# Eight uneven pieces of the first modulation weights in place of six

## The chip, the core and the metric

The kernel runs on one core of one Trainium2 chip. The core has five engines that run their own instruction streams: TensorE (PE, with its weight loads, PEld), VectorE (DVE), ScalarE (ACT), GpSimd (POOL) and SyncE (SP). Sixteen DMA engines bring data from HBM to the on-chip memory, SBUF, which has 128 partitions; here SP alone issues these transfers. The metric is the device time of one execution in microseconds.

## The reference

One token passes through a transformer block whose normalisations are modulated by a condition `c`. Everything is float32; H = 32 heads, 8192 cached keys and values of 192 numbers a head, D = 640.

```python
mod = (_silu(c) @ w_mod).reshape(c.shape[0], 6, 1, -1)
sa, ca, ga, sb, cb, gb = (mod[:, 0], mod[:, 1], mod[:, 2], mod[:, 3], mod[:, 4], mod[:, 5])
h = _layernorm(x, axis=-1) * (1 + ca) + sa
x = x + ga * _A_ref(h, A_k_cache, A_v_cache, A_wq, A_wo)   # attention of one query over the cache
h = _layernorm(x, axis=-1) * (1 + cb) + sb
x = x + gb * _B_ref(h, B_w1, B_b1, B_w2, B_b2)             # squared-relu feed-forward
```

The cache is 2 x 32 x 8192 x 192 x 4 bytes, 403 MB, and is read once. Together with the weights 451.83 MB come in.

## The kernel before

The host lays the inputs out as the transfers want them. Keys, values and the slices of `wq` and `wo` that go with them are cut by `plan()` into 53 chunks of at most 64,512 bytes a partition; each chunk is one transfer over 128 partitions, the last one two. Three buffers of this size (the pool `strm`) go round. SP's program is the list of transfers in the order written: `wm0`, the uneven pieces, chunks 0 and 1 (`load(0)`, `load(1)`), chunk 2 once the first buffer is free, and from then on `load(n + 3)` at the end of the work on chunk n; behind the chunks the remaining modulation weights (`wm1`), `w1` and `w2`, in pieces. In between, for each chunk, DVE multiplies the keys with the query (L273) and adds up the products (L281, with POOL's help at L399), PE forms the weighted sums of values (L322).

The first buffer holds, in columns, the modulation weights for the first normalisation (`wm0`: shift and scale, 2 x 640 outputs over 640 inputs, in KB = 5 groups of 128 inputs), the first slice of `wq` and some small vectors. A part of the fifth group, 480 of its 1280 columns for each of its 128 inputs, is not in this rectangle. Each of these 128 strips of 480 numbers stands at one of up to seven places (SX = 7 slots) of one of up to 64 partitions at the end of the same buffer, `wm0x_t`. DVE and POOL fill that region with zeros first (L120, L121), and then a table `XP` says where strips go. Its entries are (first partition, number of rows, slots): an entry (a, k, n) is one transfer to the k partitions a, a + 4, a + 8 and so on, each a row of n strips of 1920 bytes (L125). The host packs the values of `c` in the same way, so that zero meets zero where no strip is.

`mod(0, 2, ...)` then forms the shift and the scale on PE: the regular part at L198, the seven slots at L204. These feed the normalisation, the first query (`query(0, ...)`, L254), and with it DVE's first multiply.

SP's transfers report their landing on eight completion counters, DMAHW0 to DMAHW7 in the built program, taken in turn. A transfer that gets a counter which an earlier transfer has used carries a wait for that earlier one's landing. SP works through its list in order: what waits there holds up all that stands behind it.

Of the kernel before, what the change touches and what calls it, by code (L numbers as in the profile page):

```python
# [38 lines left out]
EXTRA = {"o": WO, "q": WQ}  # L39
SLOT = 84 * DH  # L40
SX = 7
XP = ((0, 3, SX), (1, 3, SX), (2, 3, SX), (3, 3, SX), (32, 3, SX), (33, 5, 5))
WX = 3 * DG
W0 = KB * 2 * D - WX
VPC = 5
# [48 lines left out]
def block_kernel(ctx: ExitStack, tc: tile.TileContext, kv, wm0, wm0x, wm1, w1, w2, out):  # L94
# [28 lines left out]
    r = 0  # L123
    for a, k, n in XP:
        nc.sync.dma_start(wm0x_t[a:a + 4 * k:4, :n * WX], wm0x[r:r + k, :n * WX])  # L125
# [395 lines left out]
```

## Time and profile before

| | us |
|---|---|
| median of 3 runs (1052.56 to 1052.58) | 1052.57 |
| span of the profiled execution, first to last instruction | 1050.6 |
| median less span: what lies around the profiled instructions | 2.0 |
| DVE busy in the span | 826.2 |
| PE busy in the span | 486.7 |
| POOL busy in the span | 190.5 |
| ACT busy in the span | 44.9 |

No time of the profiled execution other than its span is listed. The page gives busy time by engine, 40 slices of the span, the DMA queues, the chain of work that ended last, and groups of instructions. The chain is followed back from the last instruction: at each step to what released it. A transfer's "us to landing" runs from its issue on SP until its landing is known, and so includes the time that it stands in the rings of the DMA engines behind earlier transfers. KB on the page are 1024 bytes; MB and GB/s are decimal.

### The profile page before, as it was taken

What the parts mean: (1) busy time and instruction counts of PE and PEld (TensorE: products, weight loads), DVE (VectorE), ACT (ScalarE), POOL (GpSimd) and SP (SyncE); (2) the same over time, 40 slices, a digit from 0 to 9 for tenths busy, and PEclk for the clock granted to TensorE, in tenths of its full rate; (3) what the DMA queues carried; (4) which work ended last, traced back from release to release, by engine and by line L of the source; (5) the groups of instructions that cost most, each with busy time, mean ns of one, the idle gap of its engine ahead of it and who ended that gap; (6) DMA issues with size and microseconds to landing.
All of it is one profiled execution on the core that took longest, in us unless ns stands there. A gap on an engine that the chain in (4) does not pass through costs nothing.

```text
span 1050.6 us, 5178 instructions
## 1 busy us (share of the span) xinstructions
PE 486.7 (46%) x2130; PEld 133.8 (13%) x2130; DVE 826.2 (79%) x405; ACT 44.9 (4%) x122; POOL 190.5 (18%) x61
## 2 busy tenths in 40 slices
PE   3253334455352363436353356345446346435287
PEld 1010001111010010101011011001001011001023
DVE  1799878876959969888697895999887977988812
ACT  0100000000000000000000000000000000000001
POOL 1113121121212211212121121122211211211200
PEclk9676576777675686767677687686777767768689
DMA  9999999999999999999999999999999999999997
GB/s 406 432 433 432 431 440 442 436 436 430 433 432 432 435 440 433 432 429 434 432 433 435 435 431 434 432 438 432 438 437 431 432 430 430 432 435 440 420 432 336
DMA packets 9142, 452.14 MB, mean 430 GB/s; under 512 B 1032, under 2 KB 1036, under 8 KB 1420
## 3 DMA queue, kind: packets, MB, share of 16 engines
q1 hardware_dynamic: 9120, 451.83, 99.4%
q8 instruction: 16, 0.26, 0.1%
q14 instruction: 6, 0.05, 0.0%
HBM read 451.83 MB, written 0.00 MB: 430 GB/s over the span
## 4 chain that ended last, share of the span: by engine, by line
DMA 56%; DVE 30%; PE 12%; ACT 1%; issue 0%; SPq 0%; DVEq 0%; ACTq 0%
DMA chunk<-in_kv 53%; DVE chunk L273 16%; DVE sc L281 12%; PE ps_o L322 6%; PE ps_q L254 2%; PE att_a L354 2%; DMA w_t<-in_w 2%; DMA wm_t<-in_wm 1%; DVE os L336 1%; DVE om L334 1%; PE att_a L356 0%; ACT p L305 0%; PE ps_mx L297 0%; PE ps_mod L198 0%; PE ps_mod L204 0%
## 5 line engine op out<-in xcount | busy, mean ns | idle before, releaser
L273 DVE TENSOR_TENSOR chunk<-chunk,qb 128x8064 f32<-128x8064 f32 (+19 forms) x81 | 419.6, 5211 | 126.7 <-DMA chunk<-in_kv 121.5
L281 DVE TENSOR_REDUCE sc<-chunk 128x25 f32<-128x4800 f32 (+21 forms) x109 | 333.8, 3096 | 0.4
L399 POOL TENSOR_TENSOR chunk<-chunk 128x1824 f32<-128x1824 f32 (+9 forms) x51 | 187.4, 3675 | 801.3 <-DVE chunk L273 552.2
L322 PE MATMUL ps_o<-chunk,p 128*32 128x512 f32 x1536 | 287.1, 716 | 68.8 <-DMA chunk<-in_kv 59.4
L297 PE MATMUL ps_mx<-ident,mp 128*128 128x128 f32 x32 | 14.6, 457 | 350.4 <-DVE mp L295 350.4
L322 PEld LDWEIGHTS ps_o<-chunk,p 128*32 128x32 f32 x1536 | 66.0, 128 | 265.1 <-issue 181.4
L354 PE MATMUL att_a<-chunk,oW 128*32 128x512 f32 x96 | 64.2, 824 | 44.9 <-ACT oW L352 44.9
L254 PE MATMUL ps_q<-chunk,ln_h 128*128 128x512 f32 x110 | 66.4, 764 | 25.9 <-DMA chunk<-in_kv 25.9
L297 PEld LDWEIGHTS ps_mx<-ident,mp 128*128 128x128 f32 x32 | 5.7, 177 | 379.5 <-DVE mp L295 310.8
L305 ACT ACTIVATE p<-sc,nm 128x256 f32<-128x256 f32 x32 | 16.2, 508 | 650.2 <-DVE nm L299 650.2
L254 PEld LDWEIGHTS ps_q<-chunk,ln_h 128*128 128x128 f32 x110 | 26.4, 251 | 63.6 <-issue 34.4
L334 DVE TENSOR_TENSOR om<-ps_o,mask 96x512 f32<-96x512 f32 x32 | 21.6, 675 | 8.9 <-PE ps_o L322 8.9
L299 DVE TENSOR_REDUCE nm<-ps_mx 128x1 f32<-128x128 f32 x32 | 9.3, 292 | 19.4 <-PE ps_mx L297 19.4
L336 DVE TENSOR_REDUCE os<-om 96x64 f32<-96x512 f32 x32 | 21.8, 682 | 1.1
L354 PEld LDWEIGHTS att_a<-chunk,oW 128*32 128x32 f32 x96 | 12.1, 141 | 81.3 <-ACT oW L352 47.6
L344 DVE TENSOR_REDUCE oT<-ps_oT 128x3 f32<-128x96 f32 x16 | 4.0, 248 | 20.9 <-PE ps_oT L340 20.9
L310 PE MATMUL ps_sum<-ident,wide 128*128 128x128 f32 x16 | 7.4, 466 | 22.4 <-ACT wide L308 22.4
L340 PE MATMUL ps_oT<-ident,os 96*128 96x96 f32 x16 | 5.0, 314 | 27.0 <-DVE os L336 27.0
L198 PE MATMUL ps_mod<-wm_t,silu 128*32 128x480 f32 (+2 forms) x78 | 9.0, 602 | 14.4 <-DVE silu L180 14.4
L356 PE MATMUL att_a<-chunk,oW 128*96 128x384 f32 x32 | 14.5, 534 | 0.0
L352 ACT ACTIVATE oW<-oT,r 128x96 f32<-128x96 f32 x16 | 5.9, 372 | 174.6 <-DVE oT L344 174.6
L255 ACT ACTIVATE qb<-ps_q 128x512 f32<-128x512 f32 x12 | 7.2, 598 | 132.0 <-PE ps_q L254 132.0
(79 smaller groups left out, 99.8 us busy)
## 6 DMA issues: line engine op xcount, KB each, us to landing
chunk<-in_kv SPq DMA_DIRECT2D x38, 8064.0 KB, 35.4
chunk<-in_kv SPq DMA_DIRECT2D x11, 8000.0 KB, 36.9
chunk<-in_kv SPq DMA_DIRECT2D x2, 7872.0 KB
chunk<-in_kv SPq DMA_DIRECT2D x1, 6144.0 KB, 22.7
wm_t<-in_wm SPq DMA_DIRECT2D x1, 4480.0 KB
wm_t<-in_wm SPq DMA_DIRECT2D x1, 4257.0 KB, 12.5
chunk<-in_kv SPq DMA_DIRECT2D x1, 3264.0 KB
chunk<-in_kv SPq DMA_DIRECT2D x1, 3072.0 KB
```

Source lines behind the costliest of these rows:

```text
L254: nc.tensor.matmul(ps, h1[:, b:b + 1].to_broadcast([P, P]), w[:, b], start=(b == 0), stop=(b == KB - 1))
L273: nc.vector.tensor_mul(pr, pr, q[:, None, :].to_broadcast([P, b - a, DH]))
L281: nc.vector.tensor_reduce(sc[:, a % SRING:a % SRING + b - a], src[:, a - first:b - first], axis=AX.X, op=ALU.add)
L297: nc.tensor.transpose(ps[:, :P], mp.to_broadcast([P, P]), ident)
L299: nc.vector.tensor_reduce(nm, ps[:, :P], axis=AX.X, op=ALU.max, negate=True)
L305: nc.scalar.activation(p, s[:, :, None].to_broadcast([P, NPOS, 32 // E]), AF.Exp, bias=nm, accum_out=sp[:, h % 2:h % 2 + 1])
L322: nc.tensor.matmul(ps_t[h][32 * g:32 * (g + 1)], p[:, E * j:E * (j + 1)].rearrange("p e r -> p (e r)"), t[:, g], start=(j == 0), stop=last)
L334: nc.vector.tensor_mul(om[:n], ps_t.pop(h)[:n].rearrange("p (d e) -> p d e", e=E), mask[:n, None, :].to_broadcast([n, ED, E]))
L336: nc.vector.tensor_reduce(os_[:n, h % 2], om[:n], axis=AX.X, op=ALU.add)
L354: nc.tensor.matmul(att_a[96:, :512], oW[:, j], w[:, j, :512], start=(first and j == 0), stop=(last and j == NV - 1))
L356: nc.tensor.matmul(att_a[:96, :NV * (D - 512)], oW.rearrange("p j r -> p (j r)"), w[:, :, 512:], start=first, stop=last)
L399: nc.gpsimd.tensor_add(half, half, kt[:, m:, DH // 2:])
```

## The change

The table `XP` gets eight entries in place of six, with other partitions, row counts and slot counts. The 128 strips are the same, and so are `wm0`, the tile, and the matmuls; the host packs by the same table.

```diff
 SX = 7
-XP = ((0, 3, SX), (1, 3, SX), (2, 3, SX), (3, 3, SX), (32, 3, SX), (33, 5, 5))
+XP = ((32, 8, 4), (33, 4, 1), (0, 3, SX), (1, 3, SX), (2, 3, SX), (3, 3, SX), (20, 2, 2), (12, 1, 4))
 WX = 3 * DG
```

Before, five transfers of three rows with seven strips (13,440 bytes a row) and one of five rows with five strips (9,600 bytes). Now one of eight rows with four strips (7,680 bytes), one of four rows with one strip (1,920), four of three rows with seven strips (13,440), one of two rows with two strips (3,840) and one of one row with four strips (7,680).

The first place where this moves instructions is the start of SP's list. `wm_t<-in_wm` is `wm0`, `wm_t<-in_wm0x` are the uneven pieces, the shapes are partitions x numbers, and in brackets stands what a transfer waits for; of before:

```order
1 L122 DMA wm_t<-in_wm 128x8514
2 L125 DMA wm_t<-in_wm0x 3x3360 [waits DVE_49,Pool_49]
3 L125 DMA wm_t<-in_wm0x 3x3360 x4
4 L125 DMA wm_t<-in_wm0x 5x2400
5 L240 DMA chunk_100<-in_kv 128x12288
6 L240 DMA chunk_102<-in_kv 128x16000 [waits DMAHW0_49]
7 L240 DMA chunk_178<-in_kv 128x16128 [waits DMAHW3_49,DMAHW4_49,DMAHW2_49,DMAHW5_49,DMAHW1_49,DMAHW6_49,DVE_49,PE_49]
8 L240 DMA chunk_193<-in_kv 128x16128 [waits DMAHW7_49,DVE_49]
```

and of the change:

```order
1 L122 DMA wm_t<-in_wm 128x8514
2 L125 DMA wm_t<-in_wm0x 8x1920 [waits DVE_49,Pool_49]
3 L125 DMA wm_t<-in_wm0x 4x480
4 L125 DMA wm_t<-in_wm0x 3x3360 x4
5 L125 DMA wm_t<-in_wm0x 2x960
6 L125 DMA wm_t<-in_wm0x 1x1920 [waits DMAHW0_49]
7 L240 DMA chunk_102<-in_kv 128x12288 [waits DMAHW1_49]
8 L240 DMA chunk_104<-in_kv 128x16000 [waits DMAHW2_49]
9 L240 DMA chunk_180<-in_kv 128x16128 [waits DMAHW4_49,DMAHW5_49,DMAHW3_49,DMAHW6_49,DMAHW0_49,DMAHW7_49,DVE_49,PE_49]
10 L240 DMA chunk_195<-in_kv 128x16128 [waits DMAHW1_49,DVE_49]
```

Before, `wm0` and the pieces take counters 0 to 6, chunk 0 takes counter 7 without a wait, and chunk 1 is the first to meet a used counter. Now `wm0` and seven pieces take all eight; the one-row piece waits for counter 0, `wm0`, chunk 0 for counter 1, the eight-row piece, and chunk 1 for counter 2, the four-row piece. From here on all transfers stand in the same order as before, each with a counter two further on.

The second place is PE's start, where L204 reads the pieces; of before:

```order
1 L198 MATMUL ps_mod_104<-wm_t,silu 32x320 [waits DMAHW0_49,DVE_49]
2 L198 MATMUL ps_mod_104<-wm_t,silu 32x320 x17
3 L198 MATMUL ps_mod_104<-wm_t,silu 32x160
4 L204 MATMUL ps_mod_104<-wm_t,silu 32x160 [waits DMAHW4_49,DMAHW5_49,DMAHW3_49,DMAHW6_49,DMAHW2_49,DMAHW1_49]
5 L204 MATMUL ps_mod_104<-wm_t,silu 32x320
```

and of the change:

```order
1 L198 MATMUL ps_mod_106<-wm_t,silu 32x320 [waits DMAHW0_49,DVE_49]
2 L198 MATMUL ps_mod_106<-wm_t,silu 32x320 x17
3 L198 MATMUL ps_mod_106<-wm_t,silu 32x160
4 L204 MATMUL ps_mod_106<-wm_t,silu 32x160 [waits DMAHW4_49,DMAHW5_49,DMAHW3_49,DMAHW6_49,DMAHW2_49,DMAHW7_49,DMAHW1_49,DMAHW0_49]
5 L204 MATMUL ps_mod_106<-wm_t,silu 32x320
```

The matmuls are the same; the first one at L204 waits for all eight pieces, where it waited for six.

## The prediction

> **What bounds the kernel now.** I read the page first: the 40 slices, the queues and the chain of waits.
>
> ```profile
> DMA  9999999999999999999999999999999999999997
> ...
> q1 hardware_dynamic: 9120, 451.83, 99.4%
> q8 instruction: 16, 0.26, 0.1%
> ...
> DMA 56%; DVE 30%; PE 12%; ACT 1%; issue 0%; SPq 0%; DVEq 0%; ACTq 0%
> DMA chunk<-in_kv 53%; DVE chunk L273 16%; DVE sc L281 12%; PE ps_o L322 6%; PE ps_q L254 2%; PE att_a L354 2%; DMA w_t<-in_w 2%; DMA wm_t<-in_wm 1%; DVE os L336 1%; DVE om L334 1%; PE att_a L356 0%; ACT p L305 0%; PE ps_mx L297 0%; PE ps_mod L198 0%; PE ps_mod L204 0%
> ```
>
> The 16 DMA engines are busy from the first slice to the last but one. DVE and PE take 42% of the chain, but only between landings. The view by stretches says it sharply:
>
> ```profile
> 60.00:560.00 500.00, 229.32 (x939) 60.69 (x940) 411.54 (x186) 18.77 (x54) 95.78 (x27) 0.71 1.00 434
> 560.00:990.00 430.00, 196.88 (x784) 50.81 (x778) 365.03 (x162) 15.46 (x46) 83.41 (x23) 0.73 1.00 434
> ```
>
> The last two columns are the DMA share and GB/s: 1.00 and 434, so 434 / 16 = 27.1 GB/s an engine and no idle for 930 us. DVE is busy 82 to 85%. A microsecond that the engines lose at the start is therefore not made up later; it is seen at the end, if it falls on the engines that end last. SP queues far ahead, too:
>
> ```profile
> chunk<-in_kv SPq DMA_DIRECT2D x38, 8064.0 KB, 35.4
> ...
> chunk<-in_kv SPq DMA_DIRECT2D x1, 6144.0 KB, 22.7
> ...
> wm_t<-in_wm SPq DMA_DIRECT2D x1, 4257.0 KB, 12.5
> ...
> wm_t<-in_wm0x SPq DMA_DIRECT2D x5, 39.4 KB
> wm_t<-in_wm0x SPq DMA_DIRECT2D x1, 46.9 KB
> ```
>
> A full chunk (8064 KB of 1024 bytes, 8.26 MB) takes 8.26 MB / 434 GB/s = 19.0 us to move but lands 35.4 us after its issue: it stands about 16 us in the rings first. SP's own rows at the start, and how long one issue takes:
>
> ```profile
> 0.73 0.39 SPq L122 DMA_DIRECT2D wm_t<-in_wm  x1
> 3.28 4.39 SPq L125 DMA_DIRECT2D wm_t<-in_wm0x  x6
> 7.72 0.44 SPq L240 DMA_DIRECT2D chunk<-in_kv  x1
> ...
> 13.24 0.34 SPq L240 DMA_DIRECT2D chunk<-in_kv  x1
> ```
>
> ```profile
> L125 SPq DMA_DIRECT2D wm_t<-in_wm0x x6: 651/652/843, 3.3 to 7.0; - x6
> ...
> L240 SPq DMA_DIRECT2D chunk<-in_kv x54: 327/328/439, 7.7 to 977.8; - x54
> ```
>
> Chunk 0 is issued at 7.72, when the engines still move wm0 (landed at 0.73 + 12.5 = 13.2). So they go from wm0 to the uneven pieces and chunk 0 without a break. Chunk 1 already waits for wm0 (issued 13.24), harmless with chunk 0 in the rings.
>
> **Which engines carry the uneven pieces.** Chunk 0 is 6.29 MB, 14.5 us at 434 GB/s. Behind wm0 alone it would land at 13.2 + 14.5 = 27.7; it landed at 7.72 + 22.7 = 30.4, 2.7 us late. All six pieces (5 x 39.4 + 46.9 KB, 0.25 MB) over 16 engines would be 0.6 us; one row of each on the same engine is 5 x 13.44 + 9.6 = 76.8 KB, and at 27.1 GB/s 2.8 us. So each row goes to one engine, and a piece of three rows loads the same three. I call these loaded, the other 13 unloaded (of which two have one row of 9.6 KB). The unloaded ones are ready for chunk 0 at 13.2, in landing times.
>
> **The change, part by part.**
>
> *Bytes and rows: nothing.* 32 + 4 + 4 x 21 + 4 + 4 = 128 slots against 130. The busiest engine has at most 7.68 + 1.92 + 4 x 13.44 + 3.84 + 7.68 = 74.9 KB against 76.8, 0.07 us less; the other two loaded ones 0.35 and 0.5 us less. PE has the same matmuls, DVE and POOL clear the same tile.
>
> *The wait: the whole price.* Each SP transfer takes one of eight completion counters in turn. The order of the change shows that wm0 and seven pieces use them up: the one-row piece (ninth) waits for counter 0, which is wm0's landing, and behind it on SP stand chunk 0 (now waiting for counter 1, the eight-row piece), chunk 1 (counter 2), and everything else. In the kernel before, the wait for wm0 cleared for chunk 1 at 13.24; now at that moment only the one-row piece is issued. It is not a 128-row transfer but a small piece, so I take the row of L125, 652 ns and some 45 ns between, 0.70 us: chunk 0 is issued at 13.94. Its own counter is free by then: the eight-row piece needs 7.68 KB / 27.1 GB/s = 0.28 us behind wm0, 13.5.
>
> Then 13 engines have an empty ring, and chunk 0 pays for a start from idle. The nearest row is wm0, the one transfer that began on empty rings: 12.5 us for 4.36 MB, of which 10.05 is movement, so 2.45 us from issue to landing beside the bytes. So on the unloaded engines chunk 0 lands at 13.94 + 2.45 + 14.5 = 30.9 where it was 27.7: **3.2 us late**. On the loaded engines nothing is lost: they move pieces until about 13.2 + 2.8 = 16.0 in landing times, and find chunk 0 in the rings at latest when the others do.
>
> Bounds of the 3.2: below, an issue as short as L240's (0.33 in place of 0.65), and data 1.0 us after issue with no further cost: the first stretch, sliced by 0.1 us, has its first bytes at 1.7, 1.0 after 0.73.
>
> ```profile
> GB/s 0 0 0 0 0 0 0 0 0 0 0 0 0 0 0 0 0 1703 1362 1362 681 0 0 0 0 341 0 0 0 0 0 0 0 0 0 341 681 3065 681 341
> ```
>
> That is a landing at 13.24 + 0.37 + 1.0 + 14.5 = 29.1 instead of 27.7: 1.4 us, with nothing for the notice of the landing. Above, an issue of 0.84 in place of 0.65 and another 0.2 for engines that start apart: 3.6 us. I take 3.2, as wm0 is the same kind of transfer from the same queue.
>
> The Trainium skill (DMA: Bandwidth & Descriptors, Anatomy of one DMA) puts one transfer at about 2.0 us and its bytes at 436 GB/s, for the other issuing path; wm0 here took 12.5 where that gives 12.0. By that rule, as an estimate, the delay would be 2.7 and not 3.2 and the time 1054.6, the upper edge of the cheap restart below. The same page (Why a DMA increments its semaphore by 16 and not by 1) says that the number of engines is the largest divisor up to 16 of the slowest dimension, which agrees with the 2.7 us above, and that a single contiguous row can be cut to use all 16; then the one-row piece would be a short issue, 0.3 us less.
>
> *Who pays at the end.* The delay counts only as far as unloaded engines are among the last. The end of the stream, 1042 to 1047 in slices of 0.125 us, and what waits for it:
>
> ```profile
> GB/s 573 307 614 225 389 430 348 553 328 532 246 205 307 410 287 287 410 205 369 369 164 451 328 184 307 307 328 287 307 266 123 61 61 41 21 0 0 0 0 0
> ```
>
> ```profile
> 1046.75 0.16 PEld L464 LDWEIGHTS ps_y<-w_t,fT 128*32 128x32 f32 x8 [0.35 <-DMA w_t<-in_w]
> 1047.30 0.33 DVE L467 TENSOR_TENSOR y<-ps_y,mods 128x160 f32<-128x160 f32 x1 [5.69 <-PE ps_y L464]
> ```
>
> Up to slice 30 (1045.75) some 300 GB/s are moved, 11 engines' worth at 27.1; then 123, 61 and at 1046.4 nothing. Only three of those eleven can be loaded ones, so at least eight unloaded engines work until 1045.75 and their last packets end near 1046.0. The 2.7 us that they were ahead at chunk 0 have shrunk to about 0.5 by the end (q8's instruction transfers, for one, take their 0.1% of the same 16 engines). So the unloaded ones had 0.5 us of slack, between 0 and 0.9: 3.2 - 0.5 = **2.7**. From this goes 0.1: the engines' starts after a break need not fall worst on those that end last. Sum +2.6 us; PE, DVE and the output behind the last landing move with it.
>
> *What is hidden.* PE's matmuls at L204 now wait for eight counters, the last one the one-row piece, landing near 16.
>
> ```profile
> 14.40 4.60 PE ps_mod L198 x36
> 19.01 3.90 PE ps_mod L204 x22
> ...
> 34.80 12.97 DVE chunk L273
> ...
> 58.03 29.30 DMA chunk<-in_kv
> ```
>
> L198 covers that until 19.0. Without this cover each microsecond would move the query and DVE's first multiply (34.80), which starts after chunk 0's new landing, 30.9, as before. Chunk 3 is issued at 58.03, when the rings still hold chunk 2: no break.
>
> **The rivals.**
>
> *The loaded engines end last (not slower).* If the engines that end last are all loaded ones and the others have 3 us to spare, the pause is filled by the loaded engines' 2.8 us of pieces, and the lighter pieces even give 0.1 to 0.5 us: 1052.1 to 1052.6. For it: chunk 0's landing is set by loaded engines, 2.7 us behind the rest. Against it: eleven engines' worth of bytes 0.6 us before the end. It decides if fewer than four engines are left in the last 3 us.
>
> *A cheap restart.* Short issue and 1.0 us to data: 1.4 - 0.5 = +0.9, 1053.5; up to +2.1 I count it as no change. For it: wm0 was the first transfer of all, and a later start may be quicker. Against: wm0's 2.45 us are the only such start that was measured.
>
> *A larger loss.* If the pause puts a second one behind it (chunk 2 or 3 issued to empty rings), 2.45 more: +5, 1057.6. Against it: 16 us of queue.
>
> *No wait in effect.* If counter 0 clears much earlier than 13.24 nothing moves, 1052.6; chunk 1's row says it doesn't.
>
> **How the numbers follow.** The profiled execution spans 1050.6 us; the median of the runs is 1052.57, 2.0 more for what lies around it. 1050.6 + 2.6 = 1053.2 for the span, and 1052.57 + 2.6 = 1055.2 for the time. Its own range is 1.4 - 0.5 = +0.9 to 3.6 - 0 = +3.6: 1053.5 to 1056.2. Two tenths of a per cent, about what a measurement of this kernel can tell from no change, are 2.1 us, so the forecast lies just beyond. Chances: the forecast 0.70 above +2.1; the cheap restart, below that, 0.13; the loaded engines 0.08, no wait 0.02; the larger loss 0.05; and 0.02 for a gain over 2.1 us, for which I see no mechanism. Slower 0.75, same 0.23, faster 0.02. The range 1053.5 to 1056.2 leaves out the loaded engines, no wait, the gain and the larger loss, 0.17.
>
> **What would show it.** In SP's rows: one piece alone at 13.2, chunk 0 at 13.9 (not 7.7), chunk 1 right behind. A hole in the DMA slices from 13 to 15. Chunk 0 landing some 17 us after its issue. DMA share 1.00 afterwards, and the last PE load at 1046.75 + 2.6 = 1049.4, its stream falling off more steeply, since now the unloaded engines end together and the loaded ones before them. Wrong: chunk 0 issued before 13; the last landing within 1 us of before; an idle stretch elsewhere.

## The result, and the profile after

| | before, us | changed, us |
|---|---|---|
| median of 6 runs | 1052.57 | 1055.79 (1055.25 to 1056.59) |
| span of the profiled execution | 1050.6 | 1053.7 |

The ratio is 1.0031, with a 95% interval of 1.0019 to 1.0042: slower by 3.2 us. The profiled execution itself took 1055.51. It was forecast at 1055.2, with 1053.5 to 1056.2 as the range.

SP's rows of the changed kernel at the start, from three stretches of its timeline (start, duration, instruction, count):

```profile
0.73 0.38 SPq L122 DMA_DIRECT2D wm_t<-in_wm  x1
3.28 4.91 SPq L125 DMA_DIRECT2D wm_t<-in_wm0x  x7
...
13.28 0.27 SPq L125 DMA_DIRECT2D wm_t<-in_wm0x  x1
13.60 0.35 SPq L240 DMA_DIRECT2D chunk<-in_kv  x1
```

Seven pieces go out one after another; the eighth waits until 13.28, and chunk 0, which went out at 7.72 before, follows at 13.60. Who waited on SP for it (total, times, longest):

```profile
SPq L125 <- DMA wm_t<-in_wm: 5.1, 1, 5.1
```

What the DMA engines started to move from 12 to 20 us, in slices of 0.2 us. First the kernel before:

```profile
GB/s 0 0 2149 607 559 313 67 134 67 67 67 2033 626 559 294 48 294 246 246 0 1229 1229 492 246 0 246 246 246 0 1229 1229 492 246 0 246 246 246 0 983 1475
```

and the changed one:

```profile
GB/s 0 38 192 173 144 0 0 202 0 202 0 0 939 1475 530 284 737 0 246 0 0 0 0 0 0 737 1475 492 492 246 246 246 0 0 737 1229 737 246 492 246
```

Bytes count in the slice in which their packet starts; one large packet of chunk 0 (49,152 bytes) counts as 246 GB/s there. Before, the large packets of chunk 0 start at 12.4, where the wm0 packets end. Now only small pieces start between 12.2 and 14.2, and the large packets begin at 14.4. The second round begins at 14.2 before (2033, eight packets), at 17.0 now (737 and 1475, nine packets up to 17.4): the first packets of chunk 0 start 2 us late, and most of them take longer than the 1.8 us of the later ones. They also drift apart: the last second-round packets start at 17.8, 18.0 and 18.2.

From 12 to 60 us, before and changed (the last two columns are DMA share and GB/s):

```profile
12.00:60.00 48.00, 17.54 (x83) 7.81 (x84) 29.23 (x23) 4.24 (x7) 5.86 (x1) 0.70 1.00 432
```

```profile
12.00:60.00 48.00, 17.50 (x82) 7.53 (x83) 28.48 (x23) 3.67 (x6) 5.87 (x1) 0.72 0.97 414
```

18 GB/s less over 48 us is 48 x 18 / 434 = 2.0 us on the average of all engines. After that the changed kernel's engines are as busy as before's, and nothing is won back:

```profile
60.00:560.00 500.00, 233.00 (x934) 61.85 (x935) 412.37 (x186) 19.33 (x56) 95.76 (x27) 0.71 1.00 434
560.00:990.00 430.00, 200.34 (x790) 51.25 (x784) 361.88 (x159) 15.46 (x46) 81.87 (x22) 0.71 1.00 434
```

The end of the stream of the changed kernel, 1045.2 to 1050.2 in slices of 0.125 us, and the last weight load behind it:

```profile
GB/s 553 328 471 287 512 307 410 307 205 410 287 348 184 348 205 225 328 184 266 225 205 225 205 205 266 205 143 164 62 41 41 61 41 20 20 0 0 0 0 0
```

```profile
1049.97 0.16 PEld L464 LDWEIGHTS ps_y<-w_t,fT 128*32 128x32 f32 x8 [0.34 <-DMA w_t<-in_w]
```

The load comes 3.22 us later than the 1046.75 of before, and what follows it (DVE's two multiplies, the output) is as long as it was. The stream dies out differently. Before, it falls from 266 to 61 GB/s in 0.25 us, and what is left behind the fall lasts half a microsecond (1045.9 to 1046.4). Here it thins out from 205 at 1048.4 to 62 at 1048.7, and what is left lasts 0.9 us, to 1049.6, with about two engines far behind the rest.

### The profile page after: what moved, and what is told of

The parts are those of the page before. It is cut to its first block, busy times and chain, and to the rows that moved or that the text cites. A ratio compares the mean times of both kernels' runs of the same rounds, so it can differ in the third digit from the quotient of the medians.

```text
span 1053.7 us, 5181 instructions
## 1 busy us (share of the span) xinstructions
PE 494.6 (47%) x2130; PEld 135.1 (13%) x2130; DVE 826.3 (78%) x405; ACT 44.9 (4%) x122; POOL 190.4 (18%) x61
## 4 chain that ended last, share of the span: by engine, by line
DMA 56%; DVE 31%; PE 12%; ACT 1%; issue 0%; SPq 0%; DVEq 0%; ACTq 0%
DMA chunk<-in_kv 53%; DVE chunk L273 16%; DVE sc L281 13%; PE ps_o L322 5%; PE att_a L354 2%; PE ps_q L254 2%; DMA w_t<-in_w 2%; DMA wm_t<-in_wm 1%; DVE os L336 1%; DVE om L334 1%; PE ps_mod L198 0%; PE att_a L356 0%; ACT p L305 0%; PE ps_mx L297 0%; PE ps_mod L204 0%
## 5 line engine op out<-in xcount | busy, mean ns | idle before, releaser
L322 PE MATMUL ps_o<-chunk,p 128*32 128x512 f32 x1536 | 292.4, 727 | 67.5 <-DMA chunk<-in_kv 57.9
L297 PE MATMUL ps_mx<-ident,mp 128*128 128x128 f32 x32 | 14.6, 456 | 351.3 <-DVE mp L295 351.3
L354 PE MATMUL att_a<-chunk,oW 128*32 128x512 f32 x96 | 67.4, 860 | 44.7 <-ACT oW L352 44.7
L305 ACT ACTIVATE p<-sc,nm 128x256 f32<-128x256 f32 x32 | 16.2, 507 | 651.2 <-DVE nm L299 651.2
L354 PEld LDWEIGHTS att_a<-chunk,oW 128*32 128x32 f32 x96 | 12.4, 144 | 81.8 <-ACT oW L352 47.5
L198 PE MATMUL ps_mod<-wm_t,silu 128*32 128x480 f32 (+2 forms) x78 | 9.6, 632 | 14.4 <-DVE silu L180 14.4
L356 PE MATMUL att_a<-chunk,oW 128*96 128x384 f32 x32 | 14.6, 539 | 0.0
```

The lines of the kernel that those rows point to most:

```text
L198: nc.tensor.matmul(ps[32 * g:32 * (g + 1), at], e[:, b:b + 1].to_broadcast([P, 32]), wg, start=(b == 0), stop=(b == KB - 1 and (wx is None ...
L297: nc.tensor.transpose(ps[:, :P], mp.to_broadcast([P, P]), ident)
L305: nc.scalar.activation(p, s[:, :, None].to_broadcast([P, NPOS, 32 // E]), AF.Exp, bias=nm, accum_out=sp[:, h % 2:h % 2 + 1])
L322: nc.tensor.matmul(ps_t[h][32 * g:32 * (g + 1)], p[:, E * j:E * (j + 1)].rearrange("p e r -> p (e r)"), t[:, g], start=(j == 0), stop=last)
L354: nc.tensor.matmul(att_a[96:, :512], oW[:, j], w[:, j, :512], start=(first and j == 0), stop=(last and j == NV - 1))
L356: nc.tensor.matmul(att_a[:96, :NV * (D - 512)], oW.rearrange("p j r -> p (j r)"), w[:, :, 512:], start=first, stop=last)
```

## The experiments

The theory: SP's list stands at a used counter, chunk 0 comes late, the rings of the DMA engines run empty near 13 us, and this loss is carried to the end. The rivals: the pieces themselves cost (shapes, partitions, number); SP's issue time for two more pieces costs; the engines with pieces end last and cover the rest.

**1. All eight pieces, no wait.** POOL issues the two with the fewest rows; its transfers have other counters.

```diff
-        nc.sync.dma_start(wm0x_t[a:a + 4 * k:4, :n * WX], wm0x[r:r + k, :n * WX])
+        queue = nc.gpsimd if k < 3 else nc.sync
+        queue.dma_start(wm0x_t[a:a + 4 * k:4, :n * WX], wm0x[r:r + k, :n * WX])
```

> All eight pieces of the change, but the two-row and the one-row piece are issued by POOL, whose transfers have counters of their own; chunk 0 is again the eighth transfer of SP and waits for nothing. The theory of the wait (chunk 0 stands behind used counters and the rings run empty): chunk 0 issued near 7.7 us, time 1052.2 to 1052.8. The rival that the pieces themselves cost (their shapes, partitions, number): as with the change, 1055.3 to 1056.6.

Measured 1052.56 (1052.35 to 1053.36), against 1052.73 of the kernel before on the same chip, ratio 0.9998 (0.9989 to 1.0008). Its timeline on SP and its stretch from 12 to 60:

```profile
7.62 0.42 SPq L241 DMA_DIRECT2D chunk<-in_kv  x1
```

```profile
12.00:60.00 48.00, 17.26 (x83) 7.53 (x84) 29.57 (x23) 4.24 (x7) 5.87 (x1) 0.70 1.00 432
```

Same rows, same partitions, same number of transfers, and the loss is gone: the pieces cost nothing that the interval of about 1 us either way would show. The two that POOL issued went in smaller packets, 64 in all, over a queue of their own (q0 on the page); experiments 2 and 4 do without this difference.

**2. Before's layout in eight pieces.**

```diff
-XP = ((0, 3, SX), (1, 3, SX), (2, 3, SX), (3, 3, SX), (32, 3, SX), (33, 5, 5))
+XP = ((0, 3, SX), (1, 3, SX), (2, 3, SX), (3, 3, SX), (32, 3, SX), (33, 3, 5), (45, 1, 5), (49, 1, 5))
```

> The rows, partitions and slots of before, but the five-row piece cut into pieces of 3, 1 and 1 rows: eight pieces, nothing else. The theory of the wait: chunk 0 issued near 13.6 us, 1055.2 to 1056.6 as with the change. The rival that the new shapes cost: 1052.5 to 1052.7. A third reading, that SP's issue time of two more pieces is what counts (2 x 0.7 us): 1054.0.

Measured 1055.27 (1055.11 to 1056.16), ratio 1.0026 (1.0016 to 1.0037), chunk 0 issued at 13.57:

```profile
13.20 0.23 SPq L125 DMA_DIRECT2D wm_t<-in_wm0x  x1
13.57 0.87 SPq L240 DMA_DIRECT2D chunk<-in_kv  x2
```

The number of pieces alone brings the loss back, with before's rows. Issue time as such (1054.0) is too little.

**3. Before's layout in seven pieces.** The five-row piece is cut into `(33, 3, 5), (45, 2, 5)`.

> The rows of before with the five-row piece cut into 3 and 2 rows: seven pieces, so that chunk 0 waits for wm0 directly, with no piece in between. The theory of the wait: chunk 0 issued at 13.25 in place of 13.60, so about 0.35 us less than with eight pieces, 1054.9 to 1056.2. Issue time alone (one more piece, 0.7 us): 1053.3. Shapes: 1052.6.

Measured 1055.44 (1054.89 to 1056.06), ratio 1.0027 (1.0016 to 1.0037). One piece too many is enough: chunk 0 itself is now the ninth transfer. It is issued at 13.28, 0.3 earlier than with eight pieces, but the time doesn't show that, so this part of the expectation wasn't met; the runs of one kernel lie more than 1 us apart. Here the trace lists how long chunk 0 took from its issue:

```profile
chunk<-in_kv SPq DMA_DIRECT2D x1, 6144.0 KB, 18.6
```

18.6 - 14.5 of movement = 4.1 us, but that is the landing on the last engine, and not the price of the restart alone. What started to move from 12 to 20 us, in slices of 0.2 us as above:

```profile
GB/s 0 0 135 67 0 202 0 0 202 0 202 1966 983 447 0 144 0 96 0 246 492 0 0 492 737 983 737 0 246 0 0 0 246 1475 1229 737 0 246 0 0
```

Thirteen engines start on chunk 0 from 14.2 to 14.8 (1966, 983 and 447, the last with three pieces in it); the other three, behind their pieces, only from 15.8 to 16.2 (246 and 492).

**4. Six pieces with the new eight-row one.** `XP = ((32, 8, 4), (0, 3, SX), (1, 3, SX), (2, 3, SX), (3, 3, SX), (33, 3, 4))`

> Six pieces, with the eight-row one of the change (8 rows of 4 strips), four of three rows and one of three rows of 4 strips in place of the last four small ones. The theory of the wait: no wait for chunk 0, and the loaded engines carry 69 KB in place of 77, 0.28 us less: 1052.2 to 1052.6. The rival that eight-row pieces or the new partitions cost: over 1055.

Measured 1052.39 (1052.17 to 1053.16), ratio 0.9998 (0.9989 to 1.0008). Six pieces meet no used counter, and in this second layout too they cost nothing that can be seen. The small gain of the lighter load isn't told apart from nothing.

**5. Three pieces of eight rows.** `XP = ((0, 8, SX), (1, 8, SX), (2, 8, 2))`

> The 128 strips in three pieces of eight rows (7, 7 and 2 strips a row): eight engines carry 30.7 KB each, 1.1 us, in place of three with 77 KB; neither chunk 0 nor chunk 1 meets a used counter. The theory (the end is set by the latest engine; the instruction transfers delay other engines than these eight): the latest lag at the end falls from the three loaded engines' to that of the rest, 0.3 to 0.6 us less, 1052.0 to 1052.5. If the eight engines are the ones that the instruction transfers delay: 0.6 more, 1053.3. If the pieces' shape costs as such: over 1055.

Measured 1053.34 (1053.06 to 1053.74) against 1052.63, ratio 1.0006 (0.9998 to 1.0015): the second number of the expectation, +0.7 us, with an interval that still holds no change. The spans of the profiled executions do not overlap, though: 1051.3 to 1051.5 us in all 11 against 1050.5 to 1051.1 in the 15 of the kernel before. Its stream ends like the changed kernel's (1042 to 1048, slices of 0.15 us):

```profile
GB/s 375 444 358 478 324 512 273 495 273 478 324 410 307 341 324 290 358 222 239 273 256 205 188 256 205 154 85 68 85 85 51 68 0 0 0 0 0 0 0 0
```

No hole at the start here, 30.7 KB on each of eight engines, and yet a thin tail: some of those eight were delayed again later. The single packets in the trace of the kernel before fit the instruction transfers as the cause: each of the 16 (q8 on the page) holds an engine for 0.9 to 1.0 us, and the chunk's packet behind it takes about 0.5 longer, some 1.4 together. Two on each of eight engines would be 2.8 us, and of the 16 engines four end at 1043.0 to 1043.9, nine at 1045.7 to 1045.9 and three at 1046.0 to 1046.4. But the trace doesn't name a packet's engine, and no run changes these transfers, so this is not shown. The result gives no reason to leave the three engines of before.

**6. A longer wait.** Twelve pieces of three rows: `XP = tuple((a, 3, 4) for a in (0, 1, 2, 3, 12, 13, 14, 15)) + tuple((a, 3, 3) for a in (32, 33, 34, 35))`.

> Twelve pieces of three rows (4 or 3 strips a row): five of them wait for used counters, chunk 0 comes behind them at 13.3 plus five issues of 0.3 to 0.7 us, 14.9 to 16.8. Theory that a later issue counts in full once the rings are empty: 1.3 to 3.2 us above the change's eight pieces, 1056.6 to 1059.0. Rival that a break has one fixed price, or that the loaded engines (84 KB each here) set the end and cover the longer wait: 1055.2 to 1056.5.

Measured 1059.14 (1059.05 to 1060.03), ratio 1.0062 (1.0049 to 1.0076), just above the theory's range. SP and the last load:

```profile
13.22 3.43 SPq L125 DMA_DIRECT2D wm_t<-in_wm0x  x5
16.70 0.89 SPq L240 DMA_DIRECT2D chunk<-in_kv  x2
```

```profile
1053.39 0.16 PEld L464 LDWEIGHTS ps_y<-w_t,fT 128*32 128x32 f32 x8 [0.35 <-DMA w_t<-in_w]
```

Chunk 0 is issued 3.1 us later than in the changed kernel and the last load comes 1053.39 - 1049.97 = 3.4 us later. In this comparison a later issue onto empty rings counts in full: no fixed price, and no cover by the engines with pieces.

**7. Chunk 0 ahead of the last two pieces.** Counter 7 is free for it; what waits for counters 0 and 1 then stands behind it.

```diff
     load(0)
+    for piece in tail:
+        nc.sync.dma_start(*piece)
     load(1)
```

(`tail` holds the two-row and the one-row piece, which the loop at L125 leaves out.)

> The eight pieces of the change, but chunk 0 is issued ahead of the two-row and the one-row piece, so it waits for nothing, and these two (waiting for counters 0 and 1) and chunk 1 come behind it. Theory of the empty rings: no hole at 13 us, but the two pieces land behind chunk 0 near 30, L204 starts at 30 in place of 19, DVE's first multiply near 46, chunk 3 is issued near 69.5 when chunk 2 has been moved by 66 to 68: a hole there, 1056.5 to 1059. Rival that only SP's waiting for counters ahead of chunk 0 costs: 1052.3 to 1052.8.

Measured 1063.21 (1062.18 to 1063.88), ratio 1.0101 (1.0086 to 1.0117): the theory's direction, more than its size. In the timeline L204 stands at L208 (a shifted line):

```profile
30.40 7.68 PE L208 MATMUL ps_mod<-wm_t,silu 64*32 64x160 f32 x28 [10.99 <-DMA wm_t<-in_wm0x]
...
49.04 0.33 SPq L244 DMA_DIRECT2D chunk<-in_kv  x1
...
72.91 0.33 SPq L244 DMA_DIRECT2D chunk<-in_kv  x1
```

```profile
45.00:50.00 5.00, 4.01 (x9) 1.47 (x7) 0.43 (x2) 0.93 (x2) 0.00 (x0) 0.91 0.18 64
...
69.00:75.00 6.00, 1.72 (x3) 0.95 (x4) 5.33 (x5) 0.60 (x2) 0.00 (x0) 0.50 0.51 172
```

Two holes in place of one: chunk 2 is issued at 49.04, when chunk 1 has been moved (DMA share 0.18 from 45 to 50), and chunk 3 at 72.91 behind chunk 2 (0.51 from 69 to 75). The expectation had only the second, because it took PE's matmuls at their old speed; they took 7.68 us here in place of 3.96. Against 434 GB/s the two holes are 4.3 and 3.6 us, together 7.9 of the 9.8 us by which the span grew (1060.4 against 1050.6); where the rest went was not traced.

No version beat the kernel before beyond its interval.

## Why the prediction was right, point by point

- *The wait is the price, bytes and rows are nothing.* Shown: experiment 1 has all pieces without the wait (0.9998 of before), experiment 2 the wait without the new pieces (1.0026, where the change has 1.0031).
- *Chunk 0 issued at 13.94.* It was 13.60. The one-row piece took 0.27 to issue, shorter than any L125 row of before; the short end of the bounds was the right one. How the row was moved can be read from the packets, of before and of the change:

```profile
DMA packets 9142, 452.14 MB, mean 430 GB/s; under 512 B 1032, under 2 KB 1036, under 8 KB 1420
```

```profile
DMA packets 9156, 452.14 MB, mean 429 GB/s; under 512 B 1039, under 2 KB 1047, under 8 KB 1442
```

  That is 7 more under 512 bytes, as many as there are more rows (27 against 20), where a row cut in 16 pieces of 480 bytes would alone add 16. So the issue was short and the row not cut. The forecast had drawn a short issue from the Trainium skill (DMA: Bandwidth & Descriptors, Why a DMA increments its semaphore by 16 and not by 1), by which a single contiguous row can be cut to use all 16 engines; this trace shows no such cut.
- *A start on empty rings costs 2.45 us, 3.2 us late in all.* For most engines this was right. With the issue at 13.60 the forecast's sum becomes 13.60 + 2.45 + 14.5 - 27.7 = 2.85. In the rows from 12 to 20 us ten engines begin their second large packet between 14.2 and 14.6 before, and nine between 17.0 and 17.4 now, 2.8 us later. The 4.1 us of experiment 3 do not speak against it, since the engines with pieces set that landing. With the 2.0 us of the Trainium skill (DMA: Bandwidth & Descriptors, Anatomy of one DMA), given for the other issuing path, the same sum would be 2.4, as an estimate; the trace shows 2.8. (The forecast's 1054.6 by that rule should read 1054.7: 1052.57 + 2.7 - 0.6.)
- *0.5 us of slack at the end, and 0.1 for luck.* The slack was there; the 0.1 is the term that failed. The steep part of the stream's end (down to 61 before, 62 now) moved from 1045.9 to 1048.7, 2.8 us, as the restart says. With 0.5 us of slack the last landing would have moved by 2.3. It moved by 3.22, because about two engines end up to 0.9 us behind the others. The forecast let the engines restart together and took off 0.1 for small differences; they restarted up to 1.2 us apart, and the latest were among those that end last. The trace doesn't name a packet's engine, but the times of single packets fit. Two of the three first packets of chunk 0 that end last do so at 17.95 and 18.27, and the last two engines finish at 1049.28 and 1049.62, both 1031.3 us later; in experiment 6 the two latest, 21.47 and 21.65, and the ends, 1052.89 and 1053.04, are both 1031.4 us apart. This is what one would see if an engine kept to the end what it lost at the restart. "Falling off more steeply" was wrong for the same reason. Why the first packets of chunk 0 take 1.8 to 3.5 us, where most of the later ones take 1.8, no run shows.
- *Hidden: L204's wait.* Right: no wait for the pieces ahead of L204 in the changed kernel. DVE's first multiply started at 35.56 in place of 34.80 and did not wait for chunk 0; most of the 0.76 is L198, which took 5.15 us in place of 4.60, and no view shows why. Experiment 7 took the cover away: the query and the first multiply came later, as described there. What the prediction did not describe is that the chunks behind them were then issued onto empty rings, twice.
- *The rivals.* A cheap restart: its short issue came true, but the second packets came 2.8 us late and not 1.4. The loaded engines ending last: refuted by the 3.2 us of the result, and by experiment 6. No wait in effect: refuted by the issue at 13.28. A second hole: not in the change, but in experiment 7.

The 0.6 us between forecast and result are thus a shorter issue (-0.3) and an uneven restart (+0.9, the rest of the sum: about 0.8 for the latest engines, and the 0.1 that was taken off). That the time came out within 0.6 is in part luck, since the two errors have opposite signs.

## What to carry to other kernels

Count the transfers on a queue against the completion counters before adding one: a small transfer that is one too many puts its wait in front of everything behind it. In this kernel, which is bound by DMA from start to end, what mattered of a wait on the issuing queue was whether the rings ran empty during it. Where they did, the loss stayed to the end, the restart cost more on top, and the engine that restarted last set the time. Split pieces freely only where the total stays within the counters, or issue the rest from a queue with its own, as experiment 1 did.

## What was not expected

- PE slowed down after standing idle: the same 28 matmuls took 3.96 us behind L198 in the kernel before, and 7.68 us in experiment 7 after 11 us of waiting. From the timeline and the stretches (the granted clock is the third column from the end) of the kernel before, where it was 1.00:

```profile
18.94 3.96 PE L204 MATMUL ps_mod<-wm_t,silu 64*32 64x160 f32 x28
```

```profile
19.00:23.00 4.00, 3.90 (x30) 1.78 (x28) 0.07 (x1) 0.00 (x0) 0.00 (x0) 1.00 0.96 418
```

and of experiment 7, where it was 0.50:

```profile
30.00:38.20 8.20, 7.68 (x28) 2.92 (x28) 0.09 (x1) 0.00 (x0) 0.00 (x0) 0.50 0.86 375
```

- How long an issue takes went by the rows more than by the wait. Pieces of three rows took 0.65 us behind a wait, too, as the shortest of experiment 6's twelve shows (minimum, median and maximum in ns):

```profile
L125 SPq DMA_DIRECT2D wm_t<-in_wm0x x12: 651/651/836, 3.3 to 16.0; - x12
```

  One-row pieces took 0.42 us right behind another issue (7.63 in experiment 2), and 0.27 and 0.23 behind a wait (the change and experiment 2).
